# Placing the units of a fused attention and bilinear kernel anew in batches 1 to 4

## Chip, cores, metric

One core of one Trainium2 chip. The metric is the device time of one execution in microseconds. "Span" is the time from the first to the last instruction in a trace; the device time is some 1.7 us longer.

## The reference

Eight batches of eight heads of attention through 32 memory slots, then a bilinear block without a nonlinearity over the 4608 tokens:

```python
a = softmax(phi, axis=2)                       # batch, head, 576 tokens, 32 slots
k_m = einsum('bhsm,bhsd->bhmd', a, k)          # v_m from v in the same way
attn = softmax(q @ k_m.T / 8)                  # over the 32 slots
x = (attn @ v_m) transposed to (4608, 512)
out = ((x @ w_a) * (x @ w_b)) @ w_out          # d_ff is 1536
```

## The kernel before

The kernel issues all instructions by hand in one order; each engine then runs its own in that order. The attention of a batch is cut into named units:

- `exp`: exponential of phi (ScalarE). `qt`: transposes of q (VectorE), two heads each.
- `ks`, `vs` or `kv`+`km`: sums of k and v over the tokens (TensorE into `pk` or `pkv`), scaled by VectorE. `kt`, `vt` or `kvt`: their transposes (TensorE into `pT`, VectorE copy into `kvT`).
- `s` or `sc`: scores (TensorE into `pscore`). `e`: exponential E (ScalarE).
- `den`: sums over the slots (TensorE into `pD`) and their logarithm L (ScalarE). `nr`: R, the exponential of minus L (ScalarE), then A = E * R: on VectorE for batches 0 and 1, on GpSimd from batch 2.
- `v`, `hv`: v_m folded into w_a and w_b (TensorE into `pva`). `x`, `hx`: its casts into `vab`, half on ScalarE and half on VectorE.

The main work is the up product. A half step makes 128 of the 1536 columns for 288 tokens: two matmuls into `pa`, two into `pb`, a cast `a_sb` of pa by ScalarE, and the product `ht` of a_sb and pb by VectorE. Units of the next batch run between half steps, in slots. The down product `po` (early chunks) or `py`, `pv`, `px` (later ones) fills TensorE in between; in a plan, `y9` means nine po.

```python
class Banks:                    # eight PSUM banks, handed out in rotation
    ...
def exp_scores(g):              # e0, e1: two exponentials each
    ...
def normalise(g, hfs=slice(0, 2)):                                   # nr0, nr1
    ...
    nc.scalar.activation(out=t["R", g][:, sl], in_=t["L", g][:, sl], func=AF.Exp, scale=-1.0)
    engine = nc.vector if b < 2 else nc.gpsimd
    engine.tensor_tensor(out=attn[b][:, g, sl], in0=t["E"][:, g, sl], in1=t["R", g][:, sl], op=ALU.mult)
    ...
def ups(steps, side=()):
    side = iter(side)
    for step in steps:
        for _ in up(*step):     # pa, pb and what follows them
            work.advance()      # two or three py, pv, px
            next(side, us[step[0]]["-"])()      # the unit of this slot
    for f in side:
        work.advance()
        f()
    ...
load(2)
...
chain(1, "exp0 exp1 y9 ks0 ...")                # batch 1, nothing beside it but po
load(3)
sum_weights()                                   # GpSimd
...
ups(half_steps(1, 1, 4), slots(2, "..."))       # batch 1, second half: side units of batch 2
for b in range(2, B):                           # batch 2: side units "second"; then "every", "last"
```

The loads, all in GpSimd's queue: ... w_a, w_b, the first third of w_out, phi, k and half of q of batch 1, the second third, the other half of q, both halves of v, the last third; then phi, k, v, q of batches 2 and 3.

The softmax here doesn't subtract the row's maximum and nothing guards it: scores larger than these inputs give would overflow.

Of the kernel before, what the change touches and what calls it, by code (L numbers as in the profile page):

```python
# [18 lines left out]
def kernel(  # L19
# [72 lines left out]
    def load(b):  # L92
        load_phi(b)
        load_k(b)
        load_v(b)
        load_q(b)
# [50 lines left out]
    def fill(n, cols=512):  # L147

        pw = banks.tile([P, 512], F32, name="pw")
        for _ in range(n):  # L150
            nc.tensor.matmul(pw[:, :cols], warm[:, :P], warm[:, :cols], start=True, stop=True)
# [437 lines left out]
    def up_half(b, i, hf, x):  # L589
        ps = banks.tile([P, HALF], F32, name=("pa", "pb")[x])  # L590
        for g in range(2):
            nc.tensor.matmul(ps, vabs[b][x][:, g, P * i:P * (i + 1)], attn[b][:, g, HALF * hf:HALF * (hf + 1)],  # L592
                             start=(g == 0), stop=(g == 1))
        if x == 0:
            if b == 0:
                n = (2 * i + hf) % 20
                a_sbs[b, i, hf] = spare[:, HALF * n:HALF * (n + 1)]
            else:
                a_sbs[b, i, hf] = apool.tile([P, HALF], F16, name="a_sb")
            nc.scalar.copy(out=a_sbs[b, i, hf], in_=ps)  # L600
        else:
            t0 = S * (b % 2) + HALF * hf
            nc.vector.tensor_tensor(out=ht[:, i, t0:t0 + HALF], in0=a_sbs.pop((b, i, hf)), in1=ps, op=ALU.mult)  # L603

    def up(b, i, hfs):
        for hf in hfs:
            up_half(b, i, hf, 0)
        if len(hfs) > 1:
            yield
        for hf in hfs:  # L610
            up_half(b, i, hf, 1)
        yield
# [5 lines that stand above are left out]
            for _ in up(*step):  # L618
                work.advance()
                next(side, us[step[0]]["-"])()  # L620
        for f in side:
            work.advance()
            f()
# [5 lines left out]
    def half_steps(b, hf, lo=0):  # L629

        return [(b, i, (hf,)) for i in range(lo, NFF)]
# [10 lines left out]
    def slots(b, names):  # L642

        def both(fs):
            return lambda: [f() for f in fs]
        def unit(n):
            if n == "fin":
                return lambda: work.pull(-work.done % NFF)
            if n == "L":
                return lambda: load(b + 2) if b + 2 < B else None  # L650
            if n[0] == "y":
                return lambda: some(int(n[1:]))
            if n[0] == "d" and n[1:].isdigit():
                return lambda: work.pull(int(n[1:]))
            return us[b + n.endswith("'") - n.endswith("_")][n.rstrip("'_")]

        return [both([unit(n) for n in x.split("+")]) for x in names.split()]
# [3 lines left out]
    def some(n):  # L661
        for _ in range(n):
            next(early, None)

    def chain(b, plan):


        for x in plan.split():
            if x[0] == "f":
                fill(int(x[1:]), 256)  # L670
            elif x[0] == "y":
                some(int(x[1:]))
            elif x[0] in "ab":
                i, _, hf = x[1:].partition(".")
                for h in ([int(hf)] if hf else (0, 1)):
                    up_half(b, int(i), h, "ab".index(x[0]))
            else:
                us[b][x]()
# [3 lines left out]
    chain(0, "v0a x0a f4 a0 a1 v0b x0b f4 b0 b1 a2 b2 v1a x1a a3 b3 a4 a5 v1b x1b a6 a7 b4 b5 v2a x2a b6 b7 a8 a9")  # L682
    load(2)
    chain(0, "v2b x2b a10 a11 b8 b9 b10 b11")
    chain(1, "exp0 exp1 y9 ks0 y3 kt0 qt0 qt1 y1 y3 ks1 qt2 s0 e0 y6 kt1 qt3 den0 y3 s1 nr0 e1 y4 y2 den1 vs0 vs1 vt0 y1 vt1 nr1 hv0a hx0a hv0b y3 hx0b y2")
    load(3)
    sum_weights()
    ups(steps(1, 0, 4), slots(1, "- hv1a+hx1a hv1b+hx1b+y1 - v1a+x1a y3+v1b x1b y3"))
    ups(half_steps(1, 0, 4), slots(1, "- v2a+x2a+v2b+x2b+qt0' - - qt1'+exp0'+qt2' exp1' - kv'+km'+y9"))
    work.plan(S + HALF, 10)  # L690
    ups(half_steps(1, 1, 4), slots(2, "- kvt qt3 sc+e0+e1 - den0+den1 nr0+nr1 v0+x0a x0b - v1+x1b x1a"))
    second = "v2_+x2a_+exp0 x2b_ exp1 - kv+km qt0 qt1 kvt qt2+qt3 sc+e0 e1+v0+x0a den0+x0b v1+x1a nr0+L x1b+exp0' den1 - nr1+v2+x2a - x2b+exp1' - kv'+km' qt0'+qt1' - qt2'+kvt'+qt3'"
    every = "- sc+e0 e1 den0 v0+x0a+x0b - - nr0+exp0' - - v1+x1a qt0' x1b+den1 exp1' - v2+x2a+x2b nr1+qt1' kv'+km' qt2' - qt3' - kvt'+L -"
    last = "sc+e0 - e1 - v0+x0b - x0a den1 - - den0 v1+x1b x1a+nr0 - - - - nr1+v2+x2a - - - - - x2b"
    for b in range(2, B):
# [37 lines left out]
```

## Time and profile before

| | before |
|---|---|
| time | 245.84 us median of 4 (245.75 to 246.15) |
| span in the profile | 244.0 us |
| busy: TensorE, VectorE, ScalarE, GpSimd | 96, 68, 64, 64% |
| transfers | saturated up to some 67 us |

Lines of the page and of the chain stand in the prediction. The columns of the timeline are start, length, engine, line, operation, what it writes and reads, sizes, count, and in brackets the idle time of the engine ahead of it and what ended it.

### The profile page before, as it was taken

To read this page: it belongs to the slowest core of one execution; us is meant where nothing else is said; L and a number is where in the kernel's file an instruction comes from. 1 tells how busy PE (TensorE), PEld (TensorE's weight loads), DVE (VectorE), ACT (ScalarE), POOL (GpSimd) and SP (SyncE) were. 2 spreads that over 40 slices of the span, in tenths; PEclk is the share of its full clock that TensorE was granted. 3 is DMA by queue.
4 is the path that set the end of the run, shared out by engine and by line. 5 is a ranking of instruction groups with operands and counts; after the bars stand their busy time and mean duration, and the time that the engine had idled before them with its cause. 6 is when DMAs were issued, how large, how long until landed. Compare 5 with 4: busy or idle time off the path is not lost.

```text
span 244.0 us, 7661 instructions
## 1 busy us (share of the span) xinstructions
PE 234.6 (96%) x3043; PEld 168.1 (69%) x3043; DVE 166.2 (68%) x401; ACT 157.2 (64%) x406; POOL 155.6 (64%) x130
## 2 busy tenths in 40 slices
PE   7989998999989999999999999999999999999993
PEld 2555654456757857767788777877787878888882
DVE  3446773568949968875994659865996676756642
ACT  2265761679598589578956768587856867565330
POOL 8722263499879629892889759892849177937001
PEclk9999999999999999999999999999999999999998
DMA  6999999999937955973159732696120403042154
GB/s 198 211 207 206 209 254 208 254 224 280 224 89 167 205 110 121 236 128 81 41 146 205 177 86 46 166 203 152 34 58 3 89 0 87 3 89 61 42 128 118
DMA packets 25044, 33.82 MB, mean 139 GB/s; under 512 B 1936, under 2 KB 19472, under 8 KB 25008
## 3 DMA queue, kind: packets, MB, share of 16 engines
q0 software_dynamic: 18288, 22.84, 50.8%
q1 hardware_dynamic: 6208, 9.70, 15.8%
q10 hardware_dynamic: 512, 0.79, 1.0%
q8 instruction: 24, 0.39, 0.7%
q14 instruction: 12, 0.10, 0.1%
HBM read 42.47 MB, written 9.44 MB: 213 GB/s over the span
## 4 chain that ended last, share of the span: by engine, by line
PE 76%; DMA 16%; DVE 3%; ACT 2%; issue 1%; POOL 0%; DVEq 0%
PE pa L592 17%; PE py L464 17%; PE pb L592 16%; PE pv L464 8%; DMA wo_sb<-in_moe_w_out_dram 7%; DMA wa_sb<-in_moe_w_a_dram 6%; PE pva L337 5%; PE px L464 4%; PE po L389 3%; DMA ht<-in_k_dram 2%; PE pkv L212 2%; PE pscore L292 1%; PE pD L314 1%; PE pT L241 1%; ACT E L305 1%
## 5 line engine op out<-in xcount | busy, mean ns | idle before, releaser
L603 DVE TENSOR_TENSOR ht<-a_sb,pb 128x288 f16<-128x288 f16 x168 | 73.2, 448 | 39.4 <-ACT a_sb L600 29.9
L592 PEld LDWEIGHTS <-vab 128*128 128x128 f16 x768 | 71.6, 98 | 27.1 <-issue 9.4
L600 ACT CAST a_sb<-pa 128x288 f16<-128x288 f32 x168 | 66.6, 407 | 26.4 <-PE pa L592 24.3
L592 PE MATMUL pa<-A,vab 128*128 128x288 f16 x384 | 75.7, 287 | 0.4 <-DVE vab L349 0.2
L592 PE MATMUL pb<-A,vab 128*128 128x288 f16 x384 | 75.0, 286 | 0.3 <-ACT vab L349 0.3
L446 POOL TENSOR_TENSOR h_sums<-ht 128x768 f16<-128x768 f16 x28 | 45.9, 1642 | 33.0 <-DVE ht L603 32.4
L464 PEld LDWEIGHTS <-h_sums 128*128 128x128 f16 x384 | 37.3, 98 | 7.0 <-issue 0.5
L349 DVE CAST vab<-pva 128x512 f16<-128x512 f32 (+1 forms) x50 | 32.3, 663 | 3.3 <-PE pva L337 2.6
L349 ACT CAST vab<-pva 128x512 f16<-128x512 f32 (+1 forms) x50 | 27.9, 581 | 9.3 <-PE pva L337 9.1
L464 PEld LDWEIGHTS <-ht 128*128 128x128 f16 x288 | 28.1, 98 | 5.7 <-issue 0.4
L464 PE MATMUL py<-w_sums,h_sums 128*128 128x256 f16 x192 | 30.4, 272 | 0.0
L446 POOL TENSOR_TENSOR h_sums<-ht,h_sums 128x768 f16<-128x768 f16 x14 | 23.0, 1642 | 1.0
L446 POOL TENSOR_TENSOR h_sums<-h_sums,ht 128x768 f16<-128x768 f16 x14 | 23.0, 1642 | 0.9
L325 POOL TENSOR_TENSOR A<-E,R 128x576 f16<-128x576 f16 x12 | 15.3, 1278 | 8.8 <-ACT R L323 8.6
L305 ACT ACTIVATE E<-pscore 128x288 f16<-128x288 f32 x32 | 11.4, 417 | 14.5 <-PE pscore L292 14.5
L464 PE MATMUL pv<-w_sums,h_sums 128*128 128x256 f16 x96 | 16.2, 273 | 0.0
L464 PE MATMUL py<-wo_sb,ht 128*128 128x256 f16 x96 | 16.0, 273 | 0.0
L471 ACT ACTIVATE u<-py 128x256 f32<-128x256 f32 x32 | 12.6, 393 | 5.2 <-PE py L464 4.9
L203 DVE STREAM_TRANSPOSE qT<-q_sb 128x288 f32<-128x288 f32 x32 | 14.3, 461 | 2.3 <-DMA q_sb<-in_q_dram 2.3
L464 PE MATMUL py<-w_sums,ht 128*128 128x256 f16 x96 | 15.5, 272 | 0.1
L464 PE MATMUL px<-wo_sb,ht 128*128 128x256 f16 x96 | 15.4, 273 | 0.0
L194 ACT ACTIVATE exp_sb<-phi_sb 128x576 f16<-128x576 f32 x16 | 11.0, 698 | 5.3 <-DMA phi_sb<-in_phi_dram 5.3
(65 smaller groups left out, 274.5 us busy)
## 6 DMA issues: line engine op xcount, KB each, us to landing
out_dram<-o_sb SPq DMA_DIRECT2D x68, 128.0 KB, 2.4
kv_sb<-in_v_dram POOLq DMA_DIRECT2D x7, 576.0 KB, 11.4
phi_sb<-in_phi_dram POOLq DMA_DIRECT2D x7, 576.0 KB, 5.2
kv_sb<-in_k_dram POOLq DMA_DIRECT2D x7, 576.0 KB, 9.0
q_sb<-in_q_dram POOLq DMA_DIRECT2D x6, 576.0 KB, 13.6
wa_sb<-in_moe_w_a_dram POOLq DMA_DIRECT2D x3, 512.0 KB, 14.4
wb_sb<-in_moe_w_b_dram POOLq DMA_DIRECT2D x3, 512.0 KB, 16.2
wo_sb<-in_moe_w_out_dram POOLq DMA_DIRECT2D x3, 512.0 KB, 18.1
```

Source lines behind the costliest of these rows:

```text
L194: nc.scalar.activation(out=t["exp"][:, 2 * z:2 * z + 2, :, :], in_=phis[b][:, 2 * z:2 * z + 2, :].rearrange("p c (i m) -> p c i m", m=M), ...
L203: nc.vector.transpose(out=t["qT"][:, hp, :].bitcast(F32), in_=qs[b][:, hp, :].bitcast(F32))
L305: nc.scalar.activation(out=Ev[:, g, :, z, :], in_=pss, func=AF.Exp, scale=1.0 / (8.0 * CS))
L325: engine.tensor_tensor(out=attn[b][:, g, sl], in0=t["E"][:, g, sl], in1=t["R", g][:, sl], op=ALU.mult)
L337: nc.tensor.matmul(t["pva", lo, z][g][0][32 * j:32 * j + 32, 0:hi - lo], t["kvT"][64 * r:64 * r + 64, 4 + g, M * j:M * j + M], w_sbs[z][64 ...
L349: engine_copy(out=vabs[b][z][:, g, lo:hi], in_=pva[:, 0:hi - lo])
L446: engine.tensor_tensor(out=out, in0=in0, in1=in1, op=op)
L464: nc.tensor.matmul(po, lhs[:, i], rhs[:, i], start=first and i == 0, stop=i == KH - 1, skip_group_check=not first)
L471: nc.scalar.mul(out=x, in_=po, mul=scale)
L592: nc.tensor.matmul(ps, vabs[b][x][:, g, P * i:P * (i + 1)], attn[b][:, g, HALF * hf:HALF * (hf + 1)], start=(g == 0), stop=(g == 1))
L600: nc.scalar.copy(out=a_sbs[b, i, hf], in_=ps)
L603: nc.vector.tensor_tensor(out=ht[:, i, t0:t0 + HALF], in0=a_sbs.pop((b, i, hf)), in1=ps, op=ALU.mult)
```

## The change

Only the order is changed: no instruction is added or removed. It has three parts. In the chain of batch 1 the units are placed anew, and both sums of k run one after the other. In the second half of batch 1 one transpose of q and the two R of batch 2 move. In batch 2 the side units of batches 3 and 4 move, above all transposes of q.

```diff
-    chain(1, "exp0 exp1 y9 ks0 y3 kt0 qt0 qt1 y1 y3 ks1 qt2 s0 e0 y6 kt1 qt3 den0 y3 s1 nr0 e1 y4 y2 den1 vs0 vs1 vt0 y1 vt1 nr1 hv0a hx0a hv0b y3 hx0b y2")
+    chain(1, "exp0 y1 exp1 y11 ks0 ks1 y1 qt0 y3 kt0 qt1 s0 e0 kt1 y6 qt2 qt3 den0 y3 s1 nr0 y4 vs0 e1 vs1 den1 y1 vt1 y2 vt0 nr1 hv0a hx0a hv0b y2 hx0b y3")
...
-    ups(half_steps(1, 1, 4), slots(2, "- kvt qt3 sc+e0+e1 - den0+den1 nr0+nr1 v0+x0a x0b - v1+x1b x1a"))
-    second = "v2_+x2a_+exp0 x2b_ exp1 - kv+km qt0 qt1 kvt qt2+qt3 sc+e0 e1+v0+x0a den0+x0b v1+x1a nr0+L x1b+exp0' den1 - nr1+v2+x2a - x2b+exp1' - kv'+km' qt0'+qt1' - qt2'+kvt'+qt3'"
+    ups(half_steps(1, 1, 4), slots(2, "qt3 kvt - sc+e0+e1 - den0+den1+nr0 - v0+nr1+x0a x0b - v1+x1b x1a"))
+    second = "v2_+x2a_+exp0 x2b_ exp1 - kv+km qt0 kvt+qt1 - qt2+qt3 sc+e0 e1+v0+x0a den0+x0b nr0+v1+x1a L x1b+exp0' - exp1' v2+x2a den1+qt0' x2b - nr1+qt1'+kv'+km' - - qt2'+kvt'+qt3'"
```

A space parts slots, `+` joins the units of one, `-` is an empty one, `'` a unit of the batch after, `_` of the batch before, `L` the loads of a later batch.

## The prediction

> **What bounds the kernel now.** I read the page first, then the chain that ended last in order of time, then the timeline of all engines from 30 to 106 us, the only stretch whose order changes.
>
> ```profile
> PE 234.6 (96%) x3043; PEld 168.1 (69%) x3043; DVE 166.2 (68%) x401; ACT 157.2 (64%) x406; POOL 155.6 (64%) x130
> PE   7989998999989999999999999999999999999993
> DMA  6999999999937955973159732696120403042154
> ```
>
> TensorE is busy nearly everywhere. No instruction is removed or added (each engine keeps its count), so only time in which TensorE waits can be won. The second row says where to look: slices are 6.1 us, and the transfers are full up to about 67 us. The chain shows where it leaves TensorE:
>
> ```profile
> 22.95 18.11 DMA wo_sb<-in_moe_w_out_dram
> 41.10 1.45 PE po L389 x6
> ...
> 68.63 0.58 ACT L L315 x2
> ...
> 69.92 0.51 ACT u L471
> 70.43 1.12 ACT R L323 x2
> ...
> 71.88 0.45 DVE ht L603
> 72.33 0.61 DVE vab L349
> ...
> 72.99 0.41 PE pva L337 x7
> ...
> 101.57 0.75 DVE qT L203 x2
> ...
> 103.41 0.47 DVE qT L203
> ...
> 104.26 0.43 PE pscore L292 x20
> ```
>
> Columns are start, length, what. Three places matter: a weight transfer until 41.1 us; a run of ScalarE and VectorE work from 67.3 to 73.0; VectorE work from 100.9 to 104.3. (A fourth, 86.4 to 87.7, lies in slots that the change leaves alone.)
>
> I size the waits from starts of successive matmuls in the timeline, not from busy time: two of pa take 0.24 us, one of po 0.216, one of py 0.109, and going from one kind to another costs 0.1 to 0.3 that no order removes. What exceeds that: 0.87 us before the first sums of k (37.23), 0.42 before the po at 41.10, 0.6 in the folds at 46.3 to 47.7; 1.6 between 66 and 73.4; 0.5 at 86.7 to 87.7; 0.9 in the scores at 103.5 to 104.6. Together 4.9 us, which is 2.0% of 245.89. A gain over 2% would need all of it.
>
> **What the Trainium skill says.** "Perfetto Trace Analysis", Identifying the Most-Contended Engine: matmul busy share is no good measure, because matmuls are pipelined. Agrees: pa has a mean of 287 ns, yet starts every 122 ns; hence my use of starts. "TensorE: Matmul & The Clock Gate", Architectural detail: ScalarE and VectorE work strictly in order. Agrees: the a_sb below starts at 71.34 straight behind the two R, though its matmuls had started at 69.69. "PSUM — Partial Sum Buffer", Specifications: eight banks per partition. The kernel hands out exactly eight in rotation, so a matmul waits for whoever still reads its bank. "DMA: Bandwidth & Descriptors", Two DMAs through the same engine are not ordered: in one queue of one DMA engine descriptors start in order. Here the transfers of GpSimd's queue up to 70 us land in the order of their issue.
>
> **Part 1, the chain of batch 1 (34 to 49 us).** Before: 9 po, sums of k of group 0, 3 po, transposes, ... Now 12 po come first, then both sums of k, then 4 po; the second transposes come ahead of the next 6 po; the sums of v are spread between po and the denominators. Twelve po end at 34.33 + 12 x 0.216 = 36.9, so the wait for k, which lands at 37.1, shrinks from 0.96 to some 0.3 us. But both orders have spent the 16 po that need only the first third of wo before the second third lands at 41.06. The earned time becomes a longer wait there; only the transposes (about 0.25 us) are now done inside it. Spreading the sums of v takes perhaps another 0.2 off the folds. TensorE should then be 0.4 to 0.5 us ahead at 47.5. The next po is number 33 in both orders, and it needs the last third of wo:
>
> ```profile
> 33.12 0.76 POOL L104 DMA_DIRECT2D wo_sb<-in_moe_w_out_dram  x1 [1.81 <-DMA wo_sb<-in_moe_w_out_dram]
> ...
> 47.69 0.39 PE L337 MATMUL pva<-wb_sb,kvT 64*32 64x256 f16 x8
> 48.01 1.25 PE L389 MATMUL po<-wo_sb,ht 128*128 128x512 f16 x5
> ```
>
> ```profile
> wo_sb<-in_moe_w_out_dram POOLq DMA_DIRECT2D x1, 512.0 KB, 14.8
> ```
>
> The fence above is the DMA view of the issue at 33.12: 33.12 + 14.8 = 47.9. Before, po 33 started at 48.01; now it can start at 47.93 at best, since the second third was followed by its matmul after 0.04. Five po follow in both orders, then the up products. **Gain of part 1: 0.08 us**, whatever happened earlier. GpSimd's own sums of the weights start behind transfers tied to the same landing, so they do not move.
>
> **Part 2, slots over batch 1, second half (62 to 76 us).** A slot is one half step (two pa, two pb, about two py) and the unit behind it. One transpose of q moves two slots up, ahead of the copy of kvT; R of group 0 moves one slot up to the denominators; R of group 1 one slot down to the folds v0. The transpose ends the scores' wait for qT at 66.2: 0.13 us, and ScalarE's run, which begins with those scores, moves with it. In ScalarE's order the change is L L L L, a10, u, R0, R1, a11, vab to L L L L, R0, a10, u, a11, R1, vab (a10, a11: the casts of half steps 10 and 11).
>
> ```profile
> 70.19 1.36 ACT L323 ACTIVATE R<-L 128x576 f16<-128x576 f32 x2
> 71.07 2.51 POOL L325 TENSOR_TENSOR A<-E,R 128x576 f16<-128x576 f16 x2 [1.81 <-ACT R L323]
> 71.34 0.51 ACT L600 CAST a_sb<-pa 128x288 f16<-128x288 f32 x1
> ...
> 73.55 0.41 PE L592 MATMUL pa<-A,vab 128*128 128x288 f16 x2
> ```
>
> Successive starts give ScalarE's real cost: R 0.575, a_sb 0.28, u 0.27. So a10 comes 0.575 - 0.13 = 0.44 later, a11 0.575 + 0.13 = 0.7 earlier, vab 0.13 earlier. Fold v0 needs the banks of a10 and of the ht product behind it: that product ends at 70.62 + 0.44 = 71.1, while the fold would want it at 70.6, so a **new wait of 0.5 us** appears. The fold v1 before waited for a11 (71.86), its ht (72.33) and a vab of VectorE (72.94). Now a11 is done at 71.15, ht at 71.6, the vab at 71.6 + 0.66 = 72.3. TensorE, delayed by the new wait, comes to v1 at 72.08 (before: 71.70 unhindered) and is through by 72.66 instead of 73.33: 0.65 ahead. The next product, pa of batch 2, needs A of both groups from GpSimd: R1 ends at 71.6, plus 0.15 to start, plus 1.25 is 73.0, against 73.55 before. So 0.5 there, and 0.1 more at the next fold, whose VectorE copies are also earlier. **Gain of part 2: 0.6 us.**
>
> **Part 3, side units of batches 3 and 4 over batch 2 (74 to 104 us).** The first ten slots only swap kvt with an empty slot; the scores behind them do not wait today (85.7), so nothing. R of group 0 goes one slot up, the denominators of group 1 three down, R of group 1 four down, the second exp three up: all off TensorE's path, in slots with ScalarE at 80 to 90% but no wait. What counts are q's transposes for batch 4: two stood behind the copies of k and v (101.57, 0.75 us for both) where VectorE was the chain; one goes three slots up into VectorE's idle time near 96, one ahead of those copies. Only the first leaves the busy stretch. It began about 99.4, when the sums arrived, and the other transpose still lies in it. So kvT, the last transpose and ht, for which the scores wait, come 0.75 - 0.34 = 0.41 us earlier relative to TensorE. Of the 0.9 us wait 0.5 stays. **Gain of part 3: 0.4 us.** The risk is A of group 1 of batch 3: R1 now comes at about 98.6 to 99.2 and GpSimd has one more sum (1.64 us) ahead of A. With the loads earlier by some 1.4 us I get A done at 100.7, and the product that needs it wants to start at 100.95.
>
> **Sum:** 0.08 + 0.6 + 0.4 = 1.08 us. After 105 us units are the same and TensorE is dense, so the shift should carry to the end: 245.89 - 1.08 = 244.8 us.
>
> **Rivals.** (a) The earned time of part 1 survives: if the last third of wo landed earlier, or po 33 did not really gate, 0.4 more, and with it up to 0.5 at 41 us: 244.0. Against it: the DMA row is full until 67 us, and the issue order is unchanged. (b) ScalarE stays the bound in part 2: the R moved below a11 delays A or the casts by as much as the earlier a11 gives, and v0's new wait eats the rest. Then only 0.13 and part 3 remain: 245.3. For it: ScalarE is 4.55 us busy of 5 between 70 and 75. Against it: a11 and the ht behind it, not the vab, held v1. (c) A of batch 3 arrives late: 0.3 to 0.6 us of part 3 lost, about 245.2; a later A would even give 246. For it: a margin of 0.2 us worked out from a shifted order. (d) All waits named vanish: 241, which would need transfers to be faster; I give it nothing much.
>
> **Range and chances.** The centre is the sum. (b) and (c) together reach 245.7, (a) 244.0; repeat runs of before spread 0.4 us. So 244.0 to 245.8. Two per cent is 4.9 us, all waits there are: faster 0.01. Slower by as much would need a new wait of 5 us, and no moved unit is longer than 1.7: slower 0.01.
>
> **What would show it.** Right: po 33 starts at 47.9 with a wait of some 0.5 us for wo before it; v0 waits about 0.5 for ht, v1 hardly; the first pa of batch 2 starts near 73.0; the scores of batch 4 start near 102.5 and take 0.4 to 0.5 less; first pa of batch 3 without a wait. Wrong: po 33 before 47.8; v1 still ending at 73.3; a wait for A at 101; or a new gap after 105 us.

## More of the kernel before

One stretch needs more: the scores of batch 4, around 103 us. The next fence is from the timeline of the kernel before.

```profile
98.67 0.82 DVE L603 TENSOR_TENSOR ht<-a_sb,pb 128x288 f16<-128x288 f16 x2 [0.85 <-ACT a_sb L600]
...
99.41 0.17 DVE L227 RECIPROCAL rphi<-pkv 128x1 f32<-128x1 f32 x1
...
101.49 0.83 DVE L203 STREAM_TRANSPOSE qT<-q_sb 128x288 f32<-128x288 f32 x2
...
102.97 0.52 DVE L242 COPY kvT<-pT 128x768 f16<-128x768 f16 x1
...
103.54 1.15 PE L292 MATMUL pscore<-qT,kvT 32*32 32x288 f16 x32
```

VectorE, idle for 0.85 us before 98.67, scales the sums from 99.41 on, and two transposes of q stand in its way before it can copy kvT.

## The result, and the profile after

The changed kernel took **244.58 us** (median of 4, 244.14 to 244.93), against 245.84 in the same comparison: ratio 0.9946, 95% interval 0.9926 to 0.9965. That is within 2%, and clear of noise. The prediction was 244.8, with 244.0 to 245.8 as its range.

```profile
span 242.4 us, 7660 instructions
PE 232.4 (96%) x3043; PEld 167.7 (69%) x3043; DVE 166.4 (69%) x401; ACT 157.1 (65%) x406; POOL 155.5 (64%) x130
```

In the page of the changed kernel TensorE has the same 3043 matmuls, 96% busy as before: neither figure tells where time was won. The starts of the same up products in both traces do:

| stretch | before, us | after, us | won | predicted |
|---|---|---|---|---|
| start to the first up product of batch 1 | 49.10 | 49.02 | 0.08 | 0.08 (part 1) |
| from there to the ninth of batch 2 | 26.89 | 26.25 | 0.64 | 0.6 (part 2) |
| from there to the first of batch 3 | 25.63 | 25.59 | 0.04 | 0 |
| from there to the ninth of batch 3, behind the scores of batch 4 | 3.01 | 2.29 | 0.72 | 0.4 (part 3) |
| from there to the end | 139.38 | 139.28 | 0.10 | 0 |

The last 0.10 is not put down to the change: that stretch takes 139.28 to 139.39 in all profiles below, whatever was changed.

**Part 1 in the timeline of the changed kernel:**

```profile
45.36 0.45 PE L255 MATMUL pk<-kv_sb,exp_sb 64*32 64x64 f16 x36 [0.25 <-DMA kv_sb<-in_v_dram]
...
47.31 0.22 DVE L276 COPY kvT<-pT 128x128 f16<-128x128 f16 x1 [0.48 <-PE pT L273]
...
47.59 0.30 PE L337 MATMUL pva<-wa_sb,kvT 64*32 64x256 f16 x8 [0.33 <-DVE kvT L276]
...
47.93 1.25 PE L389 MATMUL po<-wo_sb,ht 128*128 128x512 f16 x5
```

Po 33 does start at 47.93, to the digit. But the wait I had expected before it, for the last third of w_out, is not there. TensorE waited earlier, in the second sum of v, for v (landed at 45.32), and then for a VectorE copy. The last third landed at 47.82.

**Part 2:**

In the kernel before the first of these lines is the second half of fold v0, the second the end of fold v1:

```profile
70.72 0.40 PE L337 MATMUL pva<-wb_sb,kvT 64*32 64x512 f16 x8
...
72.99 0.41 PE L337 MATMUL pva<-wb_sb,kvT 64*32 64x512 f16 x7 [0.19 <-DVE vab L349]
```

In the changed kernel:

```profile
69.40 0.78 ACT L323 ACTIVATE R<-L 128x576 f16<-128x576 f32 x1
...
69.98 0.50 ACT L600 CAST a_sb<-pa 128x288 f16<-128x288 f32 x1
...
70.51 1.03 DVE L603 TENSOR_TENSOR ht<-a_sb,pb 128x288 f16<-128x288 f16 x2 [1.56 <-ACT a_sb L600]
70.53 0.89 PE L337 MATMUL pva<-wb_sb,kvT 64*32 64x512 f16 x8
...
71.71 1.28 POOL L325 TENSOR_TENSOR A<-E,R 128x576 f16<-128x576 f16 x1 [0.16 <-ACT R L323]
...
72.23 0.40 PE L337 MATMUL pva<-wb_sb,kvT 64*32 64x512 f16 x8
...
72.79 0.53 PE L592 MATMUL pa<-A,vab 128*128 128x288 f16 x2
```

R of group 0 comes first, a10 behind it. The second half of fold v0 takes 0.89 instead of 0.40: the new wait, 0.48 us, for the ht behind a10. Fold v1 no longer waits (its second half, at 72.23, takes 0.40). A of group 1 runs from 71.71 to 72.99, and the first two up products of batch 2, begun at 72.79, take 0.53 instead of 0.41: the second of them needs that A (the run p2_r1 below shows this wait).

**Part 3**, to be read against the lines of before above:

```profile
95.33 0.47 DVE L203 STREAM_TRANSPOSE qT<-q_sb 128x288 f32<-128x288 f32 x1
...
98.09 0.47 DVE L203 STREAM_TRANSPOSE qT<-q_sb 128x288 f32<-128x288 f32 x1
...
98.66 0.17 DVE L227 RECIPROCAL rphi<-pkv 128x1 f32<-128x1 f32 x1
...
101.50 0.52 DVE L242 COPY kvT<-pT 128x768 f16<-128x768 f16 x1
...
102.59 0.63 PE L292 MATMUL pscore<-qT,kvT 32*32 32x288 f16 x32
```

From the reciprocal to the copy of kvT it is 2.84 us, against 3.56. Both transposes are out of that stretch: the second ends at 98.56, and the sums that the reciprocal waits for are not there before.

### The profile page after: what moved, and what is told of

It is laid out like the page before. It is cut to its first block, busy times and chain, and to the rows that moved or that the text cites. A ratio compares the mean times of both kernels' runs of the same rounds, so it can differ in the third digit from the quotient of the medians.

```text
span 242.4 us, 7660 instructions
## 1 busy us (share of the span) xinstructions
PE 232.4 (96%) x3043; PEld 167.7 (69%) x3043; DVE 166.4 (69%) x401; ACT 157.1 (65%) x406; POOL 155.5 (64%) x130
## 4 chain that ended last, share of the span: by engine, by line
PE 76%; DMA 17%; ACT 2%; DVE 1%; POOL 1%; issue 1%; DVEq 0%
PE pa L592 18%; PE py L464 17%; PE pb L592 17%; PE pv L464 8%; DMA wb_sb<-in_moe_w_b_dram 8%; DMA kv_sb<-in_v_dram 6%; PE pva L337 5%; PE px L464 4%; DMA ht<-in_k_dram 2%; PE pkv L212 2%; PE po L389 2%; PE pD L314 1%; PE pscore L292 1%; PE pT L241 1%; ACT E L305 1%
## 5 line engine op out<-in xcount | busy, mean ns | idle before, releaser
L315 ACT ACTIVATE L<-pD 128x288 f32<-128x288 f32 x32 | 11.4, 424 | 5.6 <-PE pD L314 5.3
```

Source lines behind the costliest of these rows:

```text
L315: nc.scalar.activation(out=t["L", g][:, sl], in_=pD, func=AF.Ln)
```

## The experiments

Times of the kernel before in the four calls were 245.63, 245.64, 245.64 and 245.64 us, on two chips; ratios are to these. Between calls only traces are compared closely. "97 to 201" is the second row of the table above, from the first up product of batch 1 to the ninth of batch 2 (numbers of matmuls into pa and pb); "289 to 297" is the fourth.

### Each part alone: p1, p2, p3

Edit: in the kernel before, only the changed line of `chain(1, ...)` (p1), of `ups(half_steps(1, 1, 4), ...)` (p2), of `second` (p3), as in the diff above.

> Part 1 alone, on the kernel before. My theory (the 33rd po cannot start before its data, so what the new order earns earlier is lost again): that po starts 0.1 us or less after or before its place in the changed kernel, 47.9 us, and the first up product of batch 1 is 0.08 us ahead of the kernel before at most; whole time within 0.2 us of before. Rival (the earned time survives, as 0.4 us): first up product 0.4 us ahead. Sub-question: in the changed kernel the sums of v were seen to wait 0.44 us for v, which I had not foreseen; that wait should be here too.

> Part 2 alone. My theory: from the first up product of batch 1 to the first of batch 2 takes 0.6 to 0.7 us less than in the kernel before (24.45 us there, 23.77 in the changed kernel), with a new wait of 0.5 us in fold v0 and none left in fold v1; whole time 0.6 to 0.7 us under before. Rival (ScalarE stays the bound): only the 0.13 us of the transpose are gained.

> Part 3 alone. From the first up product of batch 3 to the ninth (behind the scores of batch 4) took 3.02 us before and 2.29 in the changed kernel. Theory now (both transposes left VectorE's busy stretch): 2.3 us here too, so 0.7 us under before in the whole time, independent of the other parts. Rival (part of the 0.72 came from GpSimd or from the shift of part 2): 2.6 us or so, 0.4 under before.

| | time, us | ratio (95%) | 97 to 201 | 289 to 297 |
|---|---|---|---|---|
| before | 245.63 | | 26.89 | 3.01 |
| p1 | 245.69 | 1.0003 (0.9991 to 1.0015) | 27.13 | 3.02 |
| p2 | 244.91 | 0.9968 (0.9955 to 0.9981) | 26.26 | 3.01 |
| p3 | 244.90 | 0.9969 (0.9956 to 0.9982) | no profile | no profile |

Part 1 wins nothing that the times show; their interval would hide 0.08. In its trace the first up product of batch 1 starts at 48.70, which is the 0.4 us ahead that the rival named. But the transfers landed as much sooner in this execution (k at 36.69; 37.10 in the kernel before), so this is no gain of the new order. Counted from the landing of the last third of w_out, po 33 starts 0.11 us behind it (47.62 after 47.51); in the kernel before it was 0.12. The other traces say the same: with the old chain it is 0.04 in p2, p2_qt and p3_one and 0.11 in p2_r1, with the new one 0.11 in the changed kernel, no_wo and t2. And p2, with the old chain, has its first up product at 49.03, against 49.02 in the changed kernel. The wait for v is in p1 as well, 0.44 us. That trace has one more gate: q of batch 2 landed later, at 59.00 (58.62 before), VectorE's transpose of it waited, and with it the ht behind it and TensorE; that is the longer 97 to 201.

Part 2 wins 0.72 in time and 0.63 in the trace; the fold waits are those of the changed kernel. Part 3 wins 0.73. The parts add up: -0.06 + 0.72 + 0.73 = 1.39 by medians, against 1.26 for the whole. The rival for part 3 (0.4 of its own, the rest from part 2 or from GpSimd) does not fit: p2 still takes 3.01 from 289 to 297, so none of the 0.72 comes from part 2, and the interval of p3 starts at 0.44 us. The profile of p3 fell in an execution of 1302.89 us and is of no use here; its four other runs lie between 244.66 and 245.22.

### Which of the two transposes: p3_one

```diff
-nr1+qt1'+kv'+km' - - qt2'+kvt'+qt3'
+nr1+kv'+km' qt1' - qt2'+kvt'+qt3'
```

> Part 3 alone, but the second transpose of q stays behind the copies of k and v; only the first goes up. If the second one ran in idle time in part 3 (the new theory), this loses its 0.35 to 0.45 us: 2.65 to 2.75 us from first to ninth product of batch 3. If the first alone gave everything, 2.3 us as in part 3.

Part 3 with one transpose back: 245.50 us median, ratio 1.001 (0.9988 to 1.0032). Two of the six executions took 246.8 to 246.9 and spoil the ratio; the other four lie between 245.27 and 245.60. From first to ninth product of batch 3 it is **2.66 us**, between 3.01 and 2.29.

```profile
99.16 0.17 DVE L227 RECIPROCAL rphi<-pkv 128x1 f32<-128x1 f32 x1 [0.49 <-PE pkv L212]
...
101.24 0.47 DVE L203 STREAM_TRANSPOSE qT<-q_sb 128x288 f32<-128x288 f32 x1
...
102.36 0.52 DVE L242 COPY kvT<-pT 128x768 f16<-128x768 f16 x1
...
103.09 0.99 PE L292 MATMUL pscore<-qT,kvT 32*32 32x288 f16 x32
```

In this timeline VectorE is idle for 0.49 us until the sums arrive, where the changed kernel has the second transpose. The transpose that stayed stands at 101.24, in the stretch, and the scores take 0.99, between the 1.15 of before and the 0.63 of after. So each of the two transposes is worth about 0.36 us, and I had counted one.

### Within part 2: p2_qt, p2_r1

```diff
-slots(2, "- kvt qt3 sc+e0+e1 - den0+den1 nr0+nr1 v0+x0a x0b ...      # before
+slots(2, "qt3 kvt - sc+e0+e1 - den0+den1 nr0+nr1 v0+x0a x0b ...      # p2_qt
+slots(2, "qt3 kvt - sc+e0+e1 - den0+den1 nr0 v0+nr1+x0a x0b ...      # p2_r1
```

> Of part 2 only the transpose of q that goes ahead of the copy of kvT. Theory: the wait for qT in the scores (0.13 us) goes and ScalarE's run starts as much earlier: 24.3 us from the first up product of batch 1 to that of batch 2, 0.13 less than before; the rest of part 2's 0.68 comes from the two R.

> Part 2 with R of group 0 left in the slot behind the denominators (ScalarE's order L, a10, u, R0, a11, R1). No new wait in fold v0 (0.5 us in part 2), but A of group 0 starts some 0.5 us later on GpSimd and A of group 1 behind it 0.3 to 0.4 later. If A gates the first up product of batch 2, the stretch takes 24.1 to 24.2 us, against 23.78 in part 2. If not, it takes 23.3 to 23.8.

| | time, us | ratio (95%) | 97 to 201 |
|---|---|---|---|
| p2_qt | 245.50 | 0.9995 (0.9983 to 1.0007) | 26.75 |
| p2_r1 | 245.26 | 0.9986 (0.9973 to 0.9999) | 26.56 |

The transpose alone: 0.14 us in the trace (predicted 0.13). With R of group 1 moved down as well: 0.33. With R of group 0 moved up too, which is the whole of part 2: 0.63. The expectation for p2_r1 named the first up product of batch 2 as the mark, and this started 23.74 us behind the first of batch 1, as early as in p2 (23.78). By the words of the expectation A would not gate. That mark was badly chosen, since only the second of the two matmuls needs A of group 1:

```profile
70.64 2.51 POOL L325 TENSOR_TENSOR A<-E,R 128x576 f16<-128x576 f16 x2 [1.66 <-ACT R L323]
...
73.21 0.28 PE L592 MATMUL pa<-A,vab 128*128 128x288 f16 x1 [0.35 <-POOL A L325]
```

In the timeline of p2_r1 both A follow each other without a pause until 73.15, and the second matmul waits for the last of them; the start of the third is 24.51 us behind the first product of batch 1, against 24.15 in p2. In this order fold v0 does not wait at all. So A gates as predicted, and the wait of 0.48 us in fold v0 is the price for an earlier A: moving R of group 0 up makes the wait and is still right, by 0.3 us.

### What gates part 1: no_wo, no_v, no_both, no_both2

All on the changed kernel, and all wrong in their results (by relative errors of 0.22 to 0.57). The landings are what to compare.

```diff
-            nc.tensor.matmul(po, ht[:, i, P * c:P * (c + 1)], wo_sb[:, i, :],
+            nc.tensor.matmul(po, ht[:, i, P * c:P * (c + 1)], wo_sb[:, i % 8, :],    # no_wo, no_both
...
-            part = (slice(0, 3, 2), slice(1, 2))[x]
+            part = (slice(0, 3, 2), slice(0, 1) if b == 1 else slice(1, 2))[x]       # no_v, no_both
```

> The changed kernel; po 33 to 48 multiply with rows of wo that are there long before, so they wait for no transfer (wrong result on purpose, same amount of work). If, as predicted, the last third of wo gates po 33, that po moves up by 0.1 to 0.5 us. If the sums of v gate it (v lands at 45.3, and from there TensorE's own order takes 2.6 us), it stays 2.6 us behind the landing of v, and first up product and whole time do not move (within 0.1 us).

> The changed kernel; the sums of v of batch 1 read k instead, which has long landed (wrong result on purpose). The wait of 0.44 us in these sums goes. If the last third of wo is the next gate, po 33 then starts 0.04 to 0.06 us behind its landing, instead of 0.11: under 0.1 us won. If wo does not gate at all, po 33 moves up by 0.4 us.

> Both together (wrong result on purpose). Theory: po 33 starts 0.3 to 0.45 us before the landing of the last third of wo, and the first up product of batch 1 is as much earlier against that landing. But the p1 run showed a third gate, the landing of q of batch 2 at 58.6 to 59.0 us, behind which VectorE's products wait; so of that lead 0.2 us or less is left at the first up product of batch 2 and in the whole time. Rival: 0.4 us are left.

> The kernel of no_both again, because its profile fell into an execution of 1027 us (its three other times, 244.4 to 244.6 us, lie on the changed kernel's). As before: po 33 starts 0.3 us or more ahead of the landing of the last third of wo if that and v are the only gates before it; 0.2 us or less of any lead is left at the first up product of batch 2, if the landing of q of batch 2 at 58.5 to 59.0 us gates.

| | time, us | v landed | last third of w_out landed | po 33 |
|---|---|---|---|---|
| changed kernel | 244.58 | 45.32 | 47.82 | 47.93 |
| no_wo | 244.39 | 45.39 | 47.90 | 48.00 |
| no_v | 244.95 | 45.32 | 47.83 | 48.37 |
| no_both | 244.50 | no profile | | |
| no_both2 | 244.27 | 45.21 | 47.71 | 47.62 |

- no_wo: po 33 stays 2.61 us behind the landing of v, as in the changed kernel (2.61). So in the changed kernel the last third of w_out does not gate it; the sums of v do. My step named the wrong transfer.
- no_v settles nothing. In its profiled execution the second half of q of batch 1 landed at 43.05, not 42.41 as in the changed kernel, and the scores of group 1 waited for its transposes. Its times are 244.07 to 245.62.
- no_both2: with neither gate po 33 starts 0.10 us before the landing, against 0.11 after it in the changed kernel. That is 0.2 us, not the 0.3 to 0.45 expected: behind the gate taken away there are the landings of k and of the second third of w_out, and the latency of the copies of kvT (0.3 us idle before the folds, as in the fence of part 1). The lead was not lost at q of batch 2, which landed at 58.54 there; the third gate of p1 holds only where that q lands late. This expectation failed too.

What stands: part 1 shows no gain in time (p1), because the chain waits for one landing after another from 37 to 48 us, and even with the last two gone 0.2 us are to be had.

### Attempts at a better version: t1, t2

t1, on the changed kernel:

```diff
-sc+e0 e1+v0+x0a den0+x0b nr0+v1+x1a L x1b+exp0' - exp1' v2+x2a den1+qt0' x2b
+sc+e0 e1 den0 v0+x0a+x0b nr0+L exp0' v1+x1a x1b+exp1' - v2+x2a+den1+qt0' x2b
```

> The changed kernel, with fold v0 of batch 3 two slots later, one slot behind the exponentials of its scores and not in the slot of the second of them, and what follows placed anew. In the changed kernel the folds at 85.7 to 86.9 us wait 0.5 us in all for ScalarE's exponentials, a_sb and the ht behind it. Theory: this wait goes, so 0.3 to 0.5 us under the changed kernel, 1.6 to 1.8 us under before. Rival: ScalarE is behind anyhow and the wait comes back in the slots after; then as the changed kernel, within 0.1 us.

244.35 us, ratio 0.9944 (0.9931 to 0.9957). Between the ninth product of batch 2 and the first of batch 3 it is 25.58 us, against 25.59 in the changed kernel. The folds no longer wait, but the up products do: 0.37 us at 86.5 and 0.20 at 91.7, each for an ht of VectorE behind a late a_sb. The rival was right; the wait moved.

t2, on the changed kernel:

```diff
+    ON_DVE = {(1, 8, 1), (1, 9, 1), (2, 10, 0)}
-            nc.scalar.copy(out=a_sbs[b, i, hf], in_=ps)
+            (nc.vector.tensor_copy if (b, i, hf) in ON_DVE else nc.scalar.copy)(out=a_sbs[b, i, hf], in_=ps)
```

> The changed kernel, with three of the casts a_sb that stand behind exponentials in ScalarE's order done by VectorE (batch 1 second half, half steps 8 and 9; batch 2 first half, half step 10), where VectorE sat idle 1.67 and 1.56 us. If ScalarE's order is what sets the first up product of batch 2, as part 2 has it, the wait of 0.37 us before the denominators goes, R of group 1 and A come some 0.5 us earlier, and with the 0.5 us in the folds of batch 3 the whole time is 0.6 to 0.9 us under the changed kernel. Rival: VectorE's own queue becomes the wait (its ht stands behind the cast): within 0.2 us of the changed kernel.

243.99 us median, correct, ratio 0.9949 (0.9927 to 0.9970). Two of six executions, 244.91 and 245.61, make the ratio no better than the changed kernel's, though their spans (242.4 and 242.3) are like those of the others (241.9 to 242.2): their extra time lies outside the program's instructions. In the trace, 97 to 201 is 26.05 (26.25 in the changed kernel) and the stretch up to batch 3 is 25.49 (25.59): 0.3 us won, half of the lower bound of what I expected.

```profile
67.69 0.65 PE L314 MATMUL pD<-E,ones 128*128 128x288 f16 x4
68.02 1.32 ACT L315 ACTIVATE L<-pD 128x288 f32<-128x288 f32 x4 [0.30 <-PE pD L314]
```

In this timeline the four denominators run through without the 0.37 us wait, but the logarithms start only 0.21 us earlier than in the changed kernel (68.23; counted from the first up product of batch 1 it is 0.12), since the denominators are not issued sooner; and the next pb waits 0.3 us for an ht behind a cast on VectorE. Each engine was half right. The version was not timed beside the changed kernel on one chip, so I call it faster by 0.3 us in the trace, and open in time.

## Why the prediction was right

- **What bounds it.** Right: only waits of TensorE changed, and the sum of those I had sized (4.9 us) could not give 2%.
- **Part 1.** The gain was in effect right (0.08 predicted, none shown by p1; the 0.08 in the table is that of the landings, 47.89 and 47.82, and p2 with the old chain has 0.07). Its step "po 33 needs the last third of wo" is true but was not what set the time: v was, 2.6 us earlier in the chain (no_wo). I had seen the sums of v run without a wait before, at 45.73, and had not asked when v lands (45.38) when the new order sends them off at 44.7. That the result fits to 0.01 us is luck: the two gates lie within 0.1 us of each other.
- **Part 2.** Right step by step: the new wait in v0 (0.5 predicted, 0.48 measured), none in v1, A at 73.0 (72.99), transpose 0.13 (0.14), whole 0.6 (0.63 to 0.64). p2_r1 shows that A gates, and shows the trade against v0 that the two moves of R make.
- **Part 3.** The mechanism was right and its size was not. The term that was mis-sized is "Only the first leaves the busy stretch ... the other transpose still lies in it", 0.41 us; it measured 0.72. The start of the stretch was right: it is when the sums arrive. What was wrong is that the other transpose lies in it. The new order puts it ahead of the reciprocal, and the 0.85 us that VectorE sat idle shortly before had room for it: it ran from 98.09 to 98.56, and the reciprocal started at 98.66. p3_one, which puts it back, gives the 0.36 us that I had missed.
- **Rivals.** (a) did not occur: the earned time of part 1 does not survive. (b) did not: p2 wins 0.63. (c) did not: A of group 1 of batch 3 ended at 100.42 and the first product of batch 3 started at 100.87 without a wait, with more room than the 0.2 us I had worked out.
- **The sum.** 0.08 + 0.6 + 0.4 = 1.08 predicted. In time it is 1.26 by medians, in the trace 1.39 (from unrounded starts) from batch 1's first up product to the ninth of batch 3. The difference is part 3.

## What to carry to other kernels

Where one engine is full, a change of order is worth the waits that it ends on that engine, less the ones that it makes: work out both from the starts of instructions, with every engine's own order in hand. Before moving work ahead, list the landing of each transfer that stands behind it; before moving a small unit away from a busy stretch, ask what its engine does until the input of that stretch arrives: a unit that stands ahead of that point in the engine's order runs in idle time, if there is enough of it. And time earned ahead of a landing is not earned.

## What the Trainium skill lacked or had wrong

- "TensorE: Matmul & The Clock Gate", Back-to-back issue gap, says that in a real stream of weight loads and matmuls the spacing for 512 columns is some 131 ns, and that 216 ns is that of an isolated matmul. Here twelve po of 512 columns in a row, each with its own weights, start 216 ns apart in the changed kernel (nine in the kernel before do too); with 256 columns it is 109. So the 131 does not fit here and the 216 does. The same page also measures 215.7 ns for back-to-back matmuls of 512 columns, which agrees.
- "TensorE: Matmul & The Clock Gate", Seeing it yourself, warns that records of the clock can't be fully trusted and that the clock has been seen stuck low for 50 us and more. Two executions here may be of this kind, and last longer: 1302.89 us (p3) and 1027.33 (no_both). The clock of 1.0 listed for them is no measurement: neither trace holds a record of the clock, and their pages lack the PEclk row that the page of the changed kernel has. In the page of p3,

```profile
L592 PE MATMUL pb<-A,vab 128*128 128x288 f16 x384 | 349.3, 1127 | 0.0
L603 DVE TENSOR_TENSOR ht<-a_sb,pb 128x288 f16<-128x288 f16 x168 | 76.3, 454 | 644.7 <-PE pb L592 627.6
```

  the mean of a pb matmul is 1127 ns against 286 in the kernel before, while VectorE's ht is as ever (454 against 448). The other executions were normal. What causes it stays open.
- "TensorEngine Tiling (Array Packing)", Key Properties, says that a change of the tiling mode drains TensorE, but no page gives its cost. From start to start it was 0.31 us from the last matmul of a fold (64 x 32 tiles, 512 columns) to an up product, 0.215 from the last one of the scores (32 x 32, 288 columns) to an up product, and 0.216 from an up product (288 columns) to a fold, in both kernels. Full matmuls of 512 and 288 columns start 0.216 and 0.122 apart, so each of the three changes added 0.09 us.
